# Forms of the first pair of batches: made at their first product instead of inside the attention, with a new instruction order

## The chip, the cores and the metric

One core of a Trainium2 chip runs the whole kernel as one program. The metric is device time in microseconds (us): the median of three runs. The engines named below are TensorE (PE; its weight loads are listed apart as PEld), VectorE (DVE), ScalarE (ACT), GpSimd (POOL) and SyncE (SP), which issues all transfers between DRAM and on-chip memory.

## What is computed

Sigmoid attention over 8 batches of 12 heads (448 positions, 64 wide), then per batch a low-rank mixing over positions and a two-layer channel network:

```python
scores = scale * np.matmul(q, k.transpose(0, 1, 3, 2)) - np.log(S)
attn = 1.0 / (1.0 + np.exp(-scores));  x = attn @ v        # heads side by side: 448 x 768 per batch
h = x.T @ U @ V                                            # rank 32
u = x + h.T
out = u + np.maximum(u @ w_ch1, 0.0) @ w_ch2               # 768 -> 3072 -> 768
```

## The kernel before

**Two stages on one TensorE.** The attention is cut into 24 *duos* (two head pairs of one batch). A duo `d` has seven score steps (group `S{d}`, line 509), each of four f32 matmuls of 64 x 64 into two PSUM banks, which ScalarE turns into a sigmoid (line 513), and seven value steps (`V{d}`, line 522). VectorE copies the result to a tile of `u` (line 533) and reduces its maximum (line 414). After three duos a batch `b` is *mixed*: its scale is found (`scale_of`, a 128 x 128 spread over the partitions on TensorE at line 390, with four small VectorE steps behind it), `u` is split into two f16 parts, transposed by a DMA (line 558), multiplied by U (seven matmuls, line 566; groups `M{b}0`, `M{b}1`) and by V (three matmuls, line 575; `N{b}0`, `N{b}1`), and VectorE adds that to `u`. Batches 0 and 1 stay on chip (`uu`); the others lie in `wt` until they are *parked* in DRAM.

**The channel network** multiplies two batches as a pair. The 2 x 2 block products are done with seven products instead of eight, so that both the weights and the inputs are needed in seven *forms* (sums and differences of blocks), each as a high and a low f16 part. One product is nine matmuls of 128 x 128 by 448 columns (line 749). An `in_quad` (group `X`) is the seven products of one unit of the first layer, with 16 VectorE steps on 128 x 448 behind them; an `out_quad` (`Y`) those of the second layer. There are 672 products. The pairs run in the order `SEGMENTS`: pair 0 with weight blocks 0 and 1, pair 1 with all four, pair 0 again with blocks 2 and 3, then pairs 2 and 3.

**Weight forms** are made once by `decode` (24 of them, groups `D{i}{n}`): integer words are loaded into `raw`, unpacked by ScalarE (line 607) and four VectorE steps (`tw<-raw`), scaled by a spread on TensorE (`ssw`, line 390), summed on GpSimd (line 623), split (ACT line 640, DVE `wt<-tw`), and stored to DRAM (`forms`). A product's weights come back from there into `wt` (1344 KB a load).

**Input forms** of a pair come from `u_form`: per chunk `c` of three, four GpSimd subtractions (line 684) give the differences 5, 6, 7 and 4, and each of the seven forms takes one ScalarE step (high part, line 680) and one VectorE step (low part, line 376, named `s_u__155` for pair 0). For pair 0 `first_forms` does this inside the attention, as soon as batches 0 and 1 are mixed, in seven form places and three temporary ones, and writes all 21 forms to DRAM (`ufar`). `forms_again` reads the 21 back at the end of the attention for the first segment, and once more for the third.

**Order.** Every step is recorded with a cost, what it reads and writes, and a wanted position; the dictionary `SHIFT` moves the position of each group. `Plan.order()` then makes one fixed list out of these, so each engine has its instructions in a set order and waits in it. Places for tiles are handed out in the same pass.

## Time and profile before

| | |
|---|---|
| median of 3 runs | 1491.05 us (1490.25 to 1492.3) |
| the profiled execution | 1495.41 us, of which its span is 1493.6 us |
| TensorE busy | 1461.9 us (98%) |
| VectorE busy | 1114.0 us (75%) |
| ScalarE busy | 646.9 us (43%) |
| GpSimd busy | 171.4 us (11%) |
| DRAM read / written | 234.09 MB / 59.87 MB |

The profile is of one execution. Busy time of TensorE is from the start of a matmul to its modelled end, and matmuls overlap; so the pace is read from the distance between starts. "Idle before" is the time in which an engine did nothing, put down to what ended it.

### The profile page before, as it was taken

The numbers are of one execution on the slowest core, as the hardware profiler recorded it, in microseconds if no ns is written. First come the engines' busy times: TensorE is split into PE (matmuls) and PEld (weight loads), VectorE is DVE, ScalarE is ACT, GpSimd is POOL, SyncE is SP. The second block draws the span as 40 slices with busy tenths as digits, with TensorE's granted clock in tenths as the row PEclk, the third lists the DMA queues.
The fourth block names the chain that finished last, engine by engine and source line by source line (L and its number), as shares of the span: only waits on it lengthen the run. The fifth ranks groups of instructions, "written<-read, shape, count | busy, mean of one in ns | idle before, by whom it ended". The sixth has DMA issues, their size and how long they took to land.

```text
span 1493.6 us, 22682 instructions
## 1 busy us (share of the span) xinstructions
PE 1461.9 (98%) x8934; PEld 718.1 (48%) x8934; DVE 1114.0 (75%) x1886; ACT 646.9 (43%) x925; POOL 171.4 (11%) x169
## 2 busy tenths in 40 slices
PE   8999999998999899999999999999999999999999
PEld 3333433344555455555555555555555555555554
DVE  3878898879999999996657668766565698666635
ACT  6988787755455455542204322431132335132200
POOL 1214122111214212210000021000000210000000
PEclk9999999999999999999999999999999999999999
DMA  8998999999769769744395367324333564233331
GB/s 278 258 279 284 266 315 284 295 277 311 255 225 357 271 219 307 251 159 149 117 338 192 111 228 253 129 72 147 134 112 111 210 234 143 80 111 132 110 129 74
DMA packets 207819, 306.46 MB, mean 205 GB/s; under 512 B 53344, under 2 KB 190688, under 8 KB 200032
## 3 DMA queue, kind: packets, MB, share of 16 engines
q1 hardware_dynamic: 207712, 305.01, 62.1%
q8 instruction: 70, 1.15, 0.3%
q14 instruction: 37, 0.30, 0.1%
HBM read 234.09 MB, written 59.87 MB: 197 GB/s over the span
## 4 chain that ended last, share of the span: by engine, by line
PE 85%; DVE 7%; DMA 4%; SPq 1%; ACT 1%; issue 1%; POOL 0%; DVEq 0%; ACTq 0%; POOLq 0%
PE banks L749 74%; PE banks L509 5%; PE banks L522 4%; DVE sp L376 2%; DMA sp<-q_in 2%; SPq L346 1%; DVE wt L376 1%; DMA raw<-w_in 1%; DVE tw L376 1%; DMA sp<-sp 1%; PE banks L566 0%; DMA parked<-wt 0%; ACT wt L640 0%; DVE uu L376 0%; DMA ufar<-sp 0%
## 5 line engine op out<-in xcount | busy, mean ns | idle before, releaser
L749 PE MATMUL banks<-sp,wt 128*128 128x448 f16 x5634 | 1092.6, 353 | 2.8 <-DVE sp L376 1.9
L749 PEld LDWEIGHTS <-wt 128*128 128x128 f16 x6048 | 592.4, 98 | 556.8 <-issue 8.3
L376 DVE SCALAR_TENSOR_TENSOR sp<-banks,fg,sp 128x448 f32<-128x448 f32 x206 | 138.7, 679 | 57.9 <-PE banks L749 55.8
L513 ACT ACTIVATE sp<-banks,bias_s 128x896 f32<-128x896 f32 x168 | 161.4, 1003 | 34.1 <-PE banks L509 33.8
L509 PE MATMUL banks<-sp 64*64 64x448 f32 x1344 | 159.7, 564 | 12.0 <-DMA sp<-q_in 7.5
L772 ACT ACTIVATE sp<-sp 128x448 f16<-128x448 f32 (+1 forms) x126 | 72.1, 574 | 220.3 <-DVE sp L376 217.7
L522 PE MATMUL banks<-sp 64*64 64x448 f32 x1344 | 149.1, 541 | 0.6 <-DVE wt L376 0.4
L623 POOL TENSOR_TENSOR tw<-tw 128x384 f32<-128x384 f32 x96 | 96.7, 1028 | 405.6 <-DVE tw L376 355.2
L376 DVE SCALAR_TENSOR_TENSOR sp<-sp 128x448 f32<-128x448 f32 (+1 forms) x191 | 118.2, 631 | 27.3 <-ACT sp L772 26.6
L786 ACT CAST sp<-sp 128x448 f16<-128x448 f32 x163 | 89.4, 564 | 87.4 <-DVE sp L376 56.4
L376 DVE SCALAR_TENSOR_TENSOR tw<-raw,tw 128x768 int32<-128x768 int32 x96 | 90.7, 954 | 10.7 <-ACT tw L607 9.5
L787 DVE TENSOR_TENSOR sp<-sp 128x448 f16<-128x448 f32 x163 | 96.0, 621 | 2.7 <-ACT sp L786 1.6
L509 PEld LDWEIGHTS banks<-sp 64*64 64x64 f32 x1344 | 52.9, 137 | 87.1 <-issue 47.2
L522 PEld LDWEIGHTS banks<-sp 64*64 64x64 f32 x1344 | 54.8, 134 | 67.4 <-issue 58.6
L791 ACT ACTIVATE sp<-banks,fg 128x448 f32<-128x448 f32 x42 | 26.4, 629 | 117.2 <-PE banks L749 117.0
L376 DVE SCALAR_TENSOR_TENSOR uu<-banks,kg__203,uu 128x448 f32<-128x448 f32 x60 | 40.5, 681 | 42.3 <-PE banks L749 41.9
L376 DVE SCALAR_TENSOR_TENSOR uu<-banks,kg__202,uu 128x448 f32<-128x448 f32 x60 | 40.5, 680 | 31.9 <-PE banks L749 31.0
L684 POOL TENSOR_TENSOR sp<-sp 128x448 f32<-128x448 f32 x23 | 28.7, 1266 | 289.3 <-DMA sp<-parked 288.6
L749 PE MATMUL banks<-tw,wt 128*128 128x448 f16 x252 | 60.7, 352 | 0.0
L772 ACT ACTIVATE sp<-banks,fg 128x448 f32<-128x448 f32 (+1 forms) x85 | 49.5, 627 | 24.7 <-PE banks L749 24.7
L607 ACT ACTIVATE tw<-raw,minus 128x768 f32<-128x768 uint16 x48 | 47.7, 1008 | 23.4 <-DVE wt L376 12.4
L376 DVE SCALAR_TENSOR_TENSOR uu<-banks,kg__201,uu 128x448 f32<-128x448 f32 x60 | 40.2, 679 | 21.4 <-PE banks L749 20.9
(272 smaller groups left out, 997.9 us busy)
## 6 DMA issues: line engine op xcount, KB each, us to landing
wt<-forms SPq DMA_DIRECT2D x96, 1344.0 KB, 6.5
forms<-wt SPq DMA_DIRECT2D x24, 1344.0 KB, 8.9
raw<-w_in SPq DMA_DIRECT2D x24, 768.0 KB, 6.8
raw<-w_in SPq DMA_DIRECT2D x48, 384.0 KB, 6.1
uu<-parked SPq DMA_DIRECT2D x48, 224.0 KB, 5.0
y_out<-uu SPq DMA_DIRECT2D x48, 224.0 KB, 2.5
sp<-k_in SPq DMA_DIRECT2D x47, 224.0 KB, 4.7
sp<-q_in SPq DMA_DIRECT2D x47, 224.0 KB, 4.8
```

Of the source, the lines that this page charges most:

```text
L376: nc.vector.scalar_tensor_tensor(out=out, in0=in0, scalar=s, in1=in1, op0=op0, op1=op1)
L509: nc.tensor.matmul(sc.x[rows_of(m), h, :S], t.x[r, 1, lo : lo + D], t.x[r, 0], start=True, stop=True)
L513: act(1.04, lambda c=c, sc=sc: nc.scalar.activation(a[c].x, sc.x[:, :, :S], AF.Sigmoid, bias=bias_s, scale=1.0 / math.sqrt(D)), [sc, "bias ...
L522: nc.tensor.matmul(av[m].x[rows_of(h), :S], vv.x[rows_of(m), m ^ x ^ 1, j, rows_of(h)], a[c].x[rows_of(m), h], start=c == 0, stop=c == 6, ...
L607: act(0.99, lambda out_=out_, low=low: nc.scalar.activation(out_(), low(), AF.Identity, bias=minus2, scale=-0.936 * 2.0 ** -35), kw + ["mi ...
L623: pool(1.08, lambda: nc.gpsimd.tensor_tensor(out=t.x[:, o], in0=t.x[:, x], in1=t.x[:, y], op=op_), kx, ko, pos + 2)
L684: pool(1.24, lambda: nc.gpsimd.tensor_tensor(out=o.x, in0=p_.x, in1=q_.x, op=ALU.subtract), [p_, q_], [o], pos)
L749: nc.tensor.matmul(bank.x[:, :S], wt[1](k, n, x), both(f)[:, y], start=start and k == i == 0, stop=k == 2 and i == 2, skip_group_check=True)
L772: act(0.57, lambda: nc.scalar.activation(o(), x(), AF.Relu, scale=sc), kx + [kf], ko, pos)
L786: act(0.57, lambda: nc.scalar.copy(both(f)[:, 0], x.x), [x], [(f, 0)], pos)
L787: dve2(0.63, lambda: nc.vector.tensor_tensor(out=both(f)[:, 1], in0=x.x, in1=both(f)[:, 0], op=ALU.subtract), [x, (f, 0)], [(f, 1)], pos)
L791: act(0.57, lambda: nc.scalar.activation(t.x, a.x[:, :S], AF.Copy, scale=s), [a, kf], [t], e)
```

## The change

The code of `u_form` is split into `u_form` (one form of one chunk) and `u_sub` (one subtraction). `first_forms` is no longer called after the second mixing. It is called where the first segment's products are laid out: the 12 subtractions are recorded there as early groups `Q5x`, `Q6x`, `Q7x`, `Q4x`, whose results are held in ten temporary places (`TEMP`, which were three, beside seven `FS`, now gone); the 21 forms (groups `T01`, `T06`, ...) are made after the tenth score step from the end, straight into places of the products; and the 21 writes to `ufar` (groups `Z`) follow. `forms_again` is left for the third segment alone. Further: where the early weight loads may go and what they wait for (`factors`), the places of `u` of batches 2 to 7, several costs that the planner uses, and all numbers of `SHIFT`.

```diff
-    mixing=-74.7, mixings=-110.3, W0s=-104.3, L0s=-107, W1s=-104.2, S0=-258.6, V0=13.4, L1s=-6.8, W2s=-45.5, S1=-204.3, V1=7.2, L2s=3, W3s=7.6,
+    mixing=-130.5, mixings=-34.9, W0s=-49.9, L0s=-49.1, W1s=-47.6, S0=-185.5, V0=-21.4, L1s=-14.3, W2s=-43.9, S1=-161.5, V1=259.7, L2s=-27.3,
...
-    TEMP = [at_("sp", (56 + i) * S, S) for i in range(3)]
-    FS = [at_("sp", (59 + i) * S, S) for i in range(7)]
+    TEMP = [at_("sp", (56 + i) * S, S) for i in range(10)]
...
-        u32s[b] = [plan.tile(f"u{b}{c}", [UU[b * NP + c]]) if b < 2 else plan.tile("u2", U2) for c in range(NP)]
+        u32s[b] = [plan.tile(f"u{b}{c}", [UU[b * NP + c]]) if b < 2 else plan.tile("u2", U2[b % 2 * NP : b % 2 * NP + NP], False) for c in range(NP)]
...
+    def u_form(fs, n, c, src, su, pos, after=()):
+        f = fs[n, c] = spot("uf")
+        act(0.66, lambda: nc.scalar.activation(both(f)[:, 0], src.x, AF.Copy, scale=su.x), [src, su], [(f, 0)], pos, after)
+        dve2(0.68, lambda: rest(both(f)[:, 1], src.x, su.x, both(f)[:, 0]), [src, su, (f, 0)], [(f, 1)], pos)
...
-    def first_forms(su, pos):
-        for c in range(3):
-            plan.group = f"T0{c}"
-            x = {(r, n): u32s[n][c + 3 * r] for r in range(2) for n in range(2)}
-            fs = {}
-            u_form(fs, c, x, su, pos + 4 * c, FS, TEMP)
-            for n in range(1, 8):
+    def first_forms(su, early, pos, after):
+        fs, t = {}, {}
+        x = {(c, r, n): u32s[n][c + 3 * r] for c in range(3) for r in range(2) for n in range(2)}
+        for i, n in enumerate((5, 6, 7, 4)):
+            for c in range(3):
+                plan.group = f"Q{n}{c}"
+                o = t[n, c] = plan.tile("ut0", TEMP)
...
+        for i, n in enumerate((1, 6, 7, 5, 2, 4, 3)):
+            plan.group = f"T0{n}"
+            for c in range(3):
+                src = {1: x[c, 0, 0], 2: x[c, 1, 0], 3: x[c, 1, 1]}.get(n) or t[n, c]
+                u_form(fs, n, c, src, su, pos + 2 * i, after)
+        for n in (1, 6, 7, 5, 2, 4, 3):
+            plan.group = f"Z{n}"
+            for c in range(3):
                 f = fs[n, c]
-                load(lambda n=n, c=c: ufar[:, n - 1, c], lambda f=f: f.x, P * S * 4, [(f, 0), (f, 1)], [("ufar", n, c)], pos + 4 * c + 1.0)
+                load(lambda n=n, c=c: ufar[:, n - 1, c], lambda f=f: f.x, P * S * 4, [(f, 0), (f, 1)], [("ufar", n, c)], pos + 60.0)
+        return fs
...
-    def factors(i, n, e, pos, after):
-        wt = plan.tile("wt", near[0], False)
+    def factors(i, n, e, pos):
+        wt = plan.tile("wt", near[0] if len(begun) > 7 else WT[1:3] if begun else WT[1:2], False)
+        after = begun[-21:-20] or (valued[-1:] if len(begun) > 7 else valued[-3:-2] if begun else scored[-WTS : len(scored) - WTS + 1])
...
-            first_forms(su, at + 7.0)
...
+        elif opening:
+            fs = first_forms(su, at - 150.0, at - LEAD, scored[-AGAIN : len(scored) - AGAIN + 1])
```

What it moves, at three places. VectorE in the middle of the attention, before the change (`s_u__155` marks a form's low part, `wt<-banks` the copy of a value step's result, `mx` its maximum):

```order
L376 SCALAR_TENSOR_TENSOR sp<-uu,s_u__155,sp 128x448
L376 SCALAR_TENSOR_TENSOR sp<-sp,s_u__155 128x448
L376 SCALAR_TENSOR_TENSOR sp<-uu,s_u__155,sp 128x448
L414 TENSOR_REDUCE mx__159<-wt 128x1
L376 SCALAR_TENSOR_TENSOR sp<-uu,s_u__155,sp 128x448
L376 SCALAR_TENSOR_TENSOR sp<-sp,s_u__155 128x448 x2
L533 COPY wt<-banks 128x448
```

VectorE at the end of the attention, after the change (`kap` marks the addition of a mixing, `s_x` a mixing's split, `32x384` the step between U and V of a mixing):

```order
L533 COPY wt<-banks 128x448
L376 SCALAR_TENSOR_TENSOR sp<-wt,s_x__136,sp 128x448
L376 SCALAR_TENSOR_TENSOR sp<-uu,s_u__155,sp 128x448 x6
L376 SCALAR_TENSOR_TENSOR sp<-sp,s_u__155 128x448 x2
L414 TENSOR_REDUCE mx__187<-wt 128x1
L533 COPY wt<-banks 128x448
L414 TENSOR_REDUCE mx__187<-wt 128x1
L376 SCALAR_TENSOR_TENSOR wt<-banks,kap__141,wt 128x448
L414 TENSOR_REDUCE mx__173<-wt 128x1
L376 SCALAR_TENSOR_TENSOR sp<-sp,s_u__155 128x448
L376 SCALAR_TENSOR_TENSOR sp<-uu,s_u__155,sp 128x448 x3
L376 SCALAR_TENSOR_TENSOR sp<-sp,s_u__155 128x448 x9
```

The 21 low parts, which stood among the copies of batches 2 and 3, now stand in two blocks among those of the last duos. ScalarE has them likewise: 18 in a row behind the sigmoid of the 158th score step, then three more.

TensorE at the end of the attention, before the change (`wt` products, `ssw` a decode's spread, `mm_x__128` the spread of the last batch's mixing):

```order
L749 MATMUL banks<-sp,wt 128x448
L522 MATMUL banks<-sp 64x448 x20
L390 MATMUL banks<-ident,ssw__117 128x128
L390 MATMUL banks<-ident,mm_x__128 128x128
L749 LDWEIGHTS wt
```

TensorE at the same place after the change:

```order
L762 MATMUL banks<-sp,wt 128x448
L390 MATMUL banks<-ident,ssw__117 128x128
L522 MATMUL banks<-sp 64x448 x8
L509 MATMUL banks<-sp 64x448 x8
L522 MATMUL banks<-sp 64x448 x20
L762 LDWEIGHTS wt
```

The two spreads directly behind the last value steps are gone from there: the decode's stands before the last nine attention steps, the last batch's behind eleven more products. In all TensorE changes between 64-row and 128-row matmuls 93 times after the change and 109 times before it.

SyncE at the end of the attention, before the change:

```order
L346 DMA sp<-ufar 128x448 x7
L558 DMA_TRANSPOSE sp<-sp 128x21x128 x2
L346 DMA sp<-ufar 128x448 x14
L346 DMA raw<-w1_in 128x3x128 x4
L346 DMA parked6<-wt 128x448 x6
```

and after it:

```order
L558 DMA_TRANSPOSE sp<-sp 128x21x128
L346 DMA ufar<-sp 128x448 x8
L346 DMA parked5<-wt 128x448
L346 DMA ufar<-sp 128x448 x12
L558 DMA_TRANSPOSE sp<-sp 128x21x128
L346 DMA ufar<-sp 128x448
```

At this place 21 reads of `ufar` have become 21 writes; the 21 writes of the middle of the attention are gone.

## Rows read from the trace of the kernel before

**Rows 1.** The page: busy time of each engine over the span.

```profile
PE 1461.9 (98%) x8934; PEld 718.1 (48%) x8934; DVE 1114.0 (75%) x1886; ACT 646.9 (43%) x925; POOL 171.4 (11%) x169
```

**Rows 2.** Busy time by stretch: from:to, length, engines, granted clock, DMA.

```profile
0.00:110.00 110.00, 101.39 (x951) 40.34 (x955) 73.42 (x136) 85.64 (x95) 20.50 (x29) 1.00 0.95 273
110.00:180.00 70.00, 65.66 (x597) 26.94 (x593) 59.61 (x108) 59.12 (x77) 23.07 (x20) 0.95 0.91 285
180.00:290.00 110.00, 106.78 (x1004) 42.43 (x1000) 94.08 (x167) 90.68 (x102) 23.12 (x24) 1.00 1.02 282
290.00:350.00 60.00, 52.43 (x389) 20.59 (x388) 49.68 (x101) 33.77 (x44) 12.23 (x12) 0.91 0.96 328
350.00:480.00 130.00, 129.48 (x689) 67.36 (x688) 124.78 (x206) 65.79 (x95) 25.63 (x24) 1.00 0.82 267
480.00:530.00 50.00, 46.22 (x243) 23.62 (x242) 45.88 (x79) 27.10 (x40) 13.87 (x13) 1.00 0.79 289
530.00:1493.00 963.00, 959.93 (x5078) 496.79 (x5075) 666.55 (x1094) 284.81 (x476) 53.04 (x48) 1.00 0.47 163
```

**Rows 3.** TensorE's timeline where pair 0's forms are made: start, length, idle before.

```profile
168.77 0.32 PE L390 MATMUL banks<-ident,mm_x__127 128*128 128x128 f32 x1 [0.90 <-DVE wt L376]
170.68 4.83 PE L509 MATMUL banks<-sp 64*64 64x448 f32 x24 [1.59 <-DMA sp<-q_in]
...
176.30 1.73 PE L509 MATMUL banks<-sp 64*64 64x448 f32 x16
177.80 0.97 PE L522 MATMUL banks<-sp 64*64 64x448 f32 x8
```

**Rows 4.** Forms, subtractions and sigmoids between 110 and 165 us: busy, mean ns.

```profile
L376 DVE SCALAR_TENSOR_TENSOR sp<-sp,s_u__155 128x448 f16<-128x448 f32 x12 | 8.7, 747 | 0.0
L376 DVE SCALAR_TENSOR_TENSOR sp<-uu,s_u__155,sp 128x448 f16<-128x448 f32 x9 | 8.2, 907 | 0.0
...
L684 POOL TENSOR_TENSOR sp<-uu 128x448 f32<-128x448 f32 x6 | 8.3, 1376 | 18.7 <-DVE uu L376 14.9 <-DVE sp L376 3.6
...
L513 ACT ACTIVATE sp<-banks,bias_s 128x896 f32<-128x896 f32 x30 | 29.1, 1002 | 3.7 <-PE banks L509 3.6
L680 ACT ACTIVATE sp<-sp,s_u__155 128x448 f16<-128x448 f32 x12 | 7.7, 661 | 0.1
L680 ACT ACTIVATE sp<-uu,s_u__155 128x448 f16<-128x448 f32 x9 | 5.9, 662 | 1.0 <-DVE s_u__155 L397 1.0
```

**Rows 5.** The same VectorE step for pair 2, beside no subtractions (880 to 925 us).

```profile
L376 DVE SCALAR_TENSOR_TENSOR sp<-sp,s_u__183 128x448 f16<-128x448 f32 x13 | 8.2, 679 | 0.0
```

**Rows 6.** TensorE's timeline: the waits at the end of the attention.

```profile
294.40 0.98 PE L509 MATMUL banks<-sp 64*64 64x448 f32 x8 [2.05 <-ACT sp L513]
...
342.31 0.32 PE L390 MATMUL banks<-ident,ssw__117 128*128 128x128 f32 x1 [2.72 <-ACT tw L615]
345.03 0.48 PE L390 MATMUL banks<-ident,mm_x__128 128*128 128x128 f32 x1 [2.40 <-DVE mm_x__128 L419]
```

**Rows 7.** VectorE between 290 and 350 us, by kind of step.

```profile
L376 DVE SCALAR_TENSOR_TENSOR sp<-wt,s_x__136,sp 128x448 f16<-128x448 f32 x6 | 5.0, 840 | 0.0
L533 DVE COPY wt<-banks 128x448 f32<-128x448 f32 x8 | 4.9, 615 | 2.1 <-PE banks L522 2.1
L376 DVE SCALAR_TENSOR_TENSOR wt<-banks,kap__139,wt 128x448 f32<-128x448 f32 x6 | 4.1, 677 | 0.9 <-PE banks L575 0.9
L414 DVE TENSOR_REDUCE mx__187<-wt 128x1 f32<-128x448 f32 x6 | 3.7, 614 | 0.1
L376 DVE SCALAR_TENSOR_TENSOR wt<-tw,s_w__125,wt 128x1152 f16<-128x1152 f32 (+1 forms) x2 | 3.2, 1608 | 0.0
```

**Rows 8.** TensorE's timeline around a spread and a mixing.

```profile
94.20 0.32 PE L390 MATMUL banks<-ident,mm_x__128 128*128 128x128 f32 x1 [0.33 <-DVE mm_x__128 L419]
...
108.51 0.66 PE L566 MATMUL banks<-sp,ua 128*128 128x384 f16 x3
```

**Rows 9.** The page: DMA issues, size, median us from issue to landing.

```profile
wt<-forms SPq DMA_DIRECT2D x96, 1344.0 KB, 6.5
```

More of the change, by code (lines that the diff above doesn't have):

```diff
@@ L360, in dve2, with act @@
         op("DVE", max(0.06, cost - 0.08), fn, reads, writes, pos, land=0.12, port=True)
-    def act(cost, fn, reads, writes, pos):
-        op("ACT", max(0.06, cost - 0.1), fn, reads, writes, pos, land=0.14)
+    def act(cost, fn, reads, writes, pos, after=()):
+        op("ACT", max(0.06, cost - 0.1), fn, reads, writes, pos, land=0.14, after=after)
     def pool(cost, fn, reads, writes, pos, after=()):
@@ L511, in duo @@
                 kq = ([qa] if 0 in hs else []) + (list(qb) if 1 in hs else [])
-                scored.append(pe(0.757, score, [(t, i) for t in kq for i in range(2)], [sc, (a[c], "place")], pos, modes=(64, 64)))
-            act(1.04, lambda c=c, sc=sc: nc.scalar.activation(a[c].x, sc.x[:, :, :S], AF.Sigmoid, bias=bias_s, scale=1.0 / math.sqrt(D)), [sc, "bias"], [a[c]], pos)
+                scored.append(pe(0.752, score, [(t, i) for t in kq for i in range(2)], [sc, (a[c], "place")], pos, modes=(64, 64)))
+            act(0.99, lambda c=c, sc=sc: nc.scalar.activation(a[c].x, sc.x[:, :, :S], AF.Sigmoid, bias=bias_s, scale=1.0 / math.sqrt(D)), [sc, "bias"], [a[c]], pos)
         plan.group = f"V{d}"
@@ L527, in duo @@
             late = at + VALUES + V_STEP * c
-            x = pe(0.757, lambda c=c: values(c), [a[c]] + [(vv, x) for x in range(3)] + (av if c else []), av, late, modes=(64, 64), after=prev)
+            x = pe(0.752, lambda c=c: values(c), [a[c]] + [(vv, x) for x in range(3)] + (av if c else []), av, late, modes=(64, 64), after=prev)
         valued.append(x)
@@ L566, in mixed @@
                     nc.tensor.matmul(tp.x[:, :384], m.rearrange("p a b -> p (a b)"), x[:, j], start=j == 0, stop=j == 6)
-            pe(1.2, mixed, [(xt, i) for i in range(3)] + ["ux"] + KUA, [tp], pos + 2.0)
+            pe(1.14, mixed, [(xt, i) for i in range(3)] + ["ux"] + KUA, [tp], pos + 2.0)
             act(0.5, lambda tp=tp, tt=tt: nc.scalar.activation(tt.x, tp.x[:, :384], AF.Copy, scale=DOWN), [tp], [tt], pos + 2.0)
@@ L707, in u_forms @@
                 x[r, n] = t
-            u_form(fs, c, x, su, at, None, None)
-        return fs
-    def first_forms(su, pos):
-        for c in range(3):
-            plan.group = f"T0{c}"
-            x = {(r, n): u32s[n][c + 3 * r] for r in range(2) for n in range(2)}
-            fs = {}
-            u_form(fs, c, x, su, pos + 4 * c, FS, TEMP)
-            for n in range(1, 8):
+            t1, t2, t3, t4 = (spot("ut") for _ in range(4))
+            u_sub(t1, x[0, 1], x[0, 0], at)
+            u_form(fs, 1, c, x[0, 0], su, at)
@@ new lines, in u_forms @@
+            u_form(fs, 5, c, t1, su, at)
+            u_sub(t2, x[1, 1], t1, at)
+            u_form(fs, 6, c, t2, su, at)
+            u_sub(t3, x[1, 1], x[0, 1], at)
+            u_form(fs, 7, c, t3, su, at)
+            u_form(fs, 2, c, x[1, 0], su, at)
+            u_sub(t4, x[1, 0], t2, at)
+            u_form(fs, 4, c, t4, su, at)
+            u_form(fs, 3, c, x[1, 1], su, at)
+        return fs
+    def first_forms(su, early, pos, after):
[5 more added lines that the diff above has]
+                o = t[n, c] = plan.tile("ut0", TEMP)
+                if n == 5:
+                    u_sub(o, x[c, 0, 1], x[c, 0, 0], early + 9 * i + 3 * c)
+                elif n == 6:
+                    u_sub(o, x[c, 1, 1], t[5, c], early + 9 * i + 3 * c)
+                elif n == 7:
+                    u_sub(o, x[c, 1, 1], x[c, 0, 1], early + 9 * i + 3 * c)
+                else:
+                    u_sub(o, x[c, 1, 0], t[6, c], pos + 10)
+        for i, n in enumerate((1, 6, 7, 5, 2, 4, 3)):
[6 more added lines that the diff above has]
+            for c in range(3):
```

125 lines of the change are left out of this document (54 added, 71 removed).

## Prediction

> **What bounds the kernel now.** I read the page first, for the busy shares. TensorE is busy 98% of the span [rows 1], so the kernel is a list of matmuls, and only what keeps them apart can be won. The same 672 products, 24 duos and 16 half mixings run after the change; nothing of this work is removed.
>
> Next, the busy time by stretch, to see where the other 2% lies [rows 2]. From 530 us on TensorE is idle for 963.00 - 959.93 = 3.1 us, and that is the end of the program. There 5078 matmuls take 959.93 us, 0.189 us each and 1.70 us for a product of nine: a floor. All that can be won lies before 530 us: idle 8.6 us up to 110 (part of it ahead of the first matmul), 4.3 between 110 and 180, 3.2 up to 290, 7.6 between 290 and 350, 0.5 up to 480, 3.8 up to 530. Two stretches also show less than the full granted clock. 0.95 over 70 us means (1 - 0.95) x 2 x 70 = 7 us at the lower level, 1.2 GHz, which cost half of that, 3.5 us, if TensorE had work throughout; 0.91 over 60 us means some 10.8 us at 1.2 GHz, at most 5.4 us. In both, TensorE had waited just before [rows 3, 6].
>
> Last, TensorE's timeline and the other engines in those stretches, for who was waited for. Between 110 and 180 us VectorE is busy 59.6 us of 70 and ScalarE 59.1 [rows 2]. TensorE waits there for VectorE steps, 0.90 us, and for a late q, 1.59 us [rows 3]. In this stretch stand the 21 forms: on VectorE 8.7 + 8.2 = 16.9 us, on ScalarE 7.7 + 5.9 = 13.6 us, and GpSimd's subtractions [rows 4]. At the end of the attention TensorE waits 2.05 us for a sigmoid, and 2.72 and 2.40 us at two spreads whose inputs ScalarE and VectorE had not finished [rows 6]. From 350 to 480 us VectorE is busy 124.8 of 130 us, 96% [rows 2]: there it is nearly a second bound.
>
> **The change part by part.** Signs are for the time: minus is a gain.
>
> *The forms leave the middle of the attention.* 16.9 us of VectorE and 13.6 us of ScalarE go from a stretch where both are 85% busy, and 21 writes of 0.23 MB with them. That stretch loses 4.3 us idle and 3.5 us to the clock, 7.8 us in all [rows 2]. The 1.59 us for q [rows 3] may stay. The twelve subtractions stay in the attention. I take -6; bounds -7.8 and 0 (another late step in the same place).
>
> *They come back at the end of the attention.* I count the new order of VectorE from the spread of batch 6's mixing to the first addition behind a product, with these rows' prices: 21 forms at 8.2/13 = 0.63 us, 13.2 [rows 5]; 4 copies and 8 reductions at 0.61, 7.4; 4 additions of mixings at 0.68, 2.7; 6 splits at 0.83, 5.0; a decode's two splits, 3.2 [rows 7]; small steps, about 2. Together 33 us. TensorE's part between the same two marks is 24 attention steps at 0.75 us (two of them start 1.50 us apart [rows 3]), 18.0 us, one product, 1.7 us, and the matmuls of a mixing and eight changes of shape, some 3: 23 us. So TensorE has to wait up to 10 us here. It needs not all of VectorE's list: the first thing that it cannot do without is the step between the two parts of batch 6's mixing, which stands behind the last form, 26 us down the list and 19 us down TensorE's: a wait of 7. ScalarE says the same: 18 forms in a row at 13.6/21 = 0.65 us are 11.7 us in which no sigmoid (29.1/30 = 0.97 us [rows 4]) is made, and the value steps of the last but one duo wait for two of these. A wait of 7 us and a stretch at 1.2 GHz behind it like those in the profile, worth 1.7 to 3.4 us, make 9.5 us. What goes from the same place: 7.6 us idle [rows 2] and about 4 for the clock (part of its 5.4 fell in idle time), since the two spreads that were waited for for 2.72 and 2.40 us [rows 6] now have nine attention steps or eleven products ahead of them. Net -2; bounds -8 (VectorE gets ahead, no wait) and +2 (the full 10 us).
>
> *What VectorE owes afterwards.* In the new order five more decodes are done by the 69th product, where there were three. By VectorE's list up to the 69th product, priced like this, it has some 17 us more to do than TensorE from batch 6's spread on, and before the change some 6; the wait at the end of the attention pays 7 to 10 of the 17, and what is left may lie beside products that need none of it. Against this, the waits between 480 and 530 us, 3.8 us [rows 2], stood where decodes were late, and with earlier decodes they have no cause. I take 0; bounds -4 and +7.
>
> *Fewer changes of shape.* 93 for 109. The row of a single spread lasts 0.32 us [rows 6], and of a spread with its way there and back some 0.3 to 0.4 is lost; half of that for each of 16 is 2.4 to 3.2 less the spreads themselves, which remain. I take -1.5; bounds 0 and -3.
>
> *Mixings sit closer.* From a mixing's spread to its first matmul the shortest case in the trace took 14.3 us, with no wait at its end [rows 8]. In the new order four of eight mixings have only about 12 us of TensorE's work between these two. Scales, splits and the transposing DMA must fit in there; if 14.3 us is what they need, each costs 2.3. I take +2; bounds 0 and +9. Behind these matmuls attention steps of the same list wait.
>
> *Transfers.* SyncE's queue loses 21 writes in the attention and has 21 writes instead of 21 reads at its end: 4.8 MB less of some 80 so far, 17 us of transfer at 285 GB/s [rows 2]. What stands behind the writes in the queue is the load of the second unit's weights, which can be issued only when the first unit's seventh product has freed the place. It lands after 6.5 us [rows 9]; nine attention steps, 6.8 us, cover it. If that cover were gone it would cost its 6.5 us. I take 0.
>
> Sum: -6 - 2 + 0 - 1.5 + 2 + 0 = -7.5 us. It is made against the profiled execution (1495.41 us, span 1493.6), which took 4.4 us more than the median; the terms are differences, so I take them from the median: 1491.05 - 7.5 = **1483.5 us**.
>
> **A rule weighed.** The low parts that are made beside GpSimd's subtractions take longer: 0.907 and 0.747 us there [rows 4] against 0.679 for the same step where no subtraction runs [rows 5]. The Trainium skill's page "SBUF — State Buffer", section "Who interferes with whom", says that VectorE instructions with two inputs on chip and GpSimd instructions that read on-chip memory exclude each other for a whole instruction. The traces agree: 21 x 0.679 = 14.3 against 16.9 us, so that 2.6 us of waiting sit in 21 steps. By that page the moved forms become cheaper, as ten of the twelve subtractions stay behind, and these would then hold up decodes and mixings instead; with the skill's rule the burst above is 13 us, with the dearer row, 0.907, it would be 19, and the wait at the end of the attention 12 instead of 7.
>
> **The rivals.** *The burst and the debt decide (slower).* The 21 forms fall where VectorE is next to full. Price: all of the 10 us wait and 3.4 for the clock at the end, the 7 of the 17 us owed by the 69th product that this wait does not pay, the closer mixings at +6: -6 + 2 + 7 - 1.5 + 6 = +7.5, and so 1498.5 us. It decides as soon as VectorE's list is more than about 8 us longer than TensorE's there. For it: 96% from 350 us on [rows 2]. Against: TensorE waited in the same place before [rows 6], and those waits go. *The waits only change places (same).* The order is new everywhere; the stretch of the forms is relieved, but other late q's and closer mixings take its 6 us: 1491 us. For it: TensorE's waits outside that stretch, 8.6 us up to 110 and 3.2 up to 290 [rows 2], are not due to forms. *Nearly all waits go (much faster).* Relieved by 17 us, VectorE is ahead when the burst comes: -7.8 - 6 - 1.5 = -15, so 1476 us. Against it: the count of the burst. That the change does not do what it says can be left out: the order shows the forms moved.
>
> **How the numbers follow.** Forecast 0.50, slower rival 0.19, same 0.16, much faster 0.15. The likeliest is 1483.5 us. Its own bounds, one wide term at a time, are 1477 to 1490. The range reaches toward the rivals until 0.1 is left out on either side: 1474 to 1497. A measurement of this kernel can tell 0.2%, 3 us, from no change: faster means below 1488. Nearly all of the forecast and all of the much faster case lie there, 0.64; within 3 us, 0.17; slower, 0.19.
>
> **What would show it.** Right: between 110 and 180 us VectorE well below 59 us busy, no lower clock there, waits below 2 us; at the end of the attention one wait of 5 to 8 us for VectorE or ScalarE with forms in front of it; no wait at the two spreads; about 31 us of TensorE's idle time down to 24. Wrong: a TensorE wait above 10 us at the forms, further waits in the first 70 products, waits at the first matmul of the mixings, or any wait beyond 530 us, where there is none now.

## The result and the profile after

The changed kernel is slower by 1%: 1506.93 us (median of 6, 1503.4 to 1513.34) against 1491.67 us for the kernel before in the same runs, a ratio of 1.0104, 95% interval [1.0081, 1.0127]. The forecast was 1483.5 us, range 1474 to 1497. The profiled execution of after took 1513.34 us (span 1511.6), the longest of its six; that of before 1495.41 (span 1493.6). A run of almost the same order, further down (r0), left a profile of 1508.19 us; where the two differ much, both are given.

Busy time of after by stretch, columns as in [rows 2], whose first six stretches are the same:

```profile
0.00:110.00 110.00, 99.56 (x928) 39.39 (x929) 71.73 (x135) 82.80 (x92) 22.40 (x29) 0.98 0.92 260
110.00:180.00 70.00, 68.12 (x647) 27.75 (x649) 60.48 (x108) 58.37 (x66) 24.05 (x22) 1.00 0.94 285
180.00:290.00 110.00, 101.01 (x924) 41.02 (x920) 82.26 (x146) 81.60 (x92) 19.37 (x20) 0.97 1.02 273
290.00:350.00 60.00, 53.26 (x426) 22.45 (x419) 55.66 (x100) 47.00 (x66) 13.02 (x12) 0.94 0.87 277
350.00:480.00 130.00, 118.07 (x597) 59.25 (x596) 118.53 (x214) 59.44 (x86) 23.36 (x23) 0.96 0.77 241
480.00:530.00 50.00, 49.75 (x265) 25.69 (x263) 43.92 (x72) 25.11 (x39) 21.37 (x16) 1.00 0.88 319
```

Set TensorE's idle time (length minus busy) beside [rows 2]: -2.5 us between 110 and 180, where the forms were made; +1.8 up to 110, +5.8 between 180 and 290, -0.8 up to 350, +11.4 between 350 and 480, -3.5 up to 530. That is +12.2 us. From 530 us on it is +1.6, nearly all of it one wait for VectorE that before did not have; apart from that both run at the floor there:

```profile
937.32 7.54 PE L762 MATMUL banks<-sp,wt 128*128 128x448 f16 x39 [1.47 <-DVE uu L376]
```

The rest of the 18.0 us between the two spans, 4.2 us, is the clock: TensorE is busy 1466.1 us instead of 1461.9 with the same matmuls. The trace shows 27.3 us at 1.2 GHz after the start of the program, in five stretches that each follow waits, where before had 17.1 in three; TensorE had work in 22.2 and 13.6 of them.

TensorE's waits in after (line, what it waited for: total us, times, longest); before had 7.5 us on the first line, 1.9 on the second (line 566, a transpose), none on the third and the fifth, 0.9 on the fourth, and 27.8 us in all where after has 41:

```profile
PE banks L509 <- DMA sp<-q_in: 10.2, 5, 4.4
PE banks L566 <- DMA sp<-sp: 9.4, 6, 4.2
PE banks L762 <- DMA wt<-forms: 5.4, 5, 1.4
PE banks L575 <- DVE sp L376: 4.4, 1, 4.4
PE banks L575 <- DVE wt L533: 3.0, 2, 2.8
```

Five places are behind most of this. First, a mixing that waits for its transpose, on TensorE's timeline (start, length, idle before it). The stretch at 1.2 GHz is the 6.8 us from 271.4 on; the 16 score matmuls that it ends in take 2.17 us instead of 1.68:

```profile
273.34 1.14 PE L566 MATMUL banks<-sp,ua 128*128 128x384 f16 x3 [4.24 <-DMA sp<-sp]
...
277.25 2.17 PE L509 MATMUL banks<-sp 64*64 64x448 f32 x16
...
286.73 1.68 PE L509 MATMUL banks<-sp 64*64 64x448 f32 x16
```

Second, SyncE's queue. At the same place two transposes hold it for 10.77 us (first row), and k and q for a later duo are issued only behind them; nobody waited for these. At 80 us TensorE did wait, for a q that was issued behind two transposes (SyncE's queue, then TensorE):

```profile
262.84 10.77 SPq L558 DMA_TRANSPOSE sp<-sp  x2
...
53.09 6.17 SPq L558 DMA_TRANSPOSE sp<-sp  x1
62.08 5.57 SPq L558 DMA_TRANSPOSE sp<-sp  x1
73.35 0.46 SPq L346 DMA_DIRECT2D sp<-q_in  x1
80.09 1.82 PE L509 MATMUL banks<-sp 64*64 64x448 f32 x8 [2.41 <-DMA sp<-q_in]
```

Third, the forms at the end of the attention: the copy out of a bank (line 533, at 311.23) stands on VectorE behind eight forms (`s_u__155`), and TensorE waits for it:

```profile
308.72 0.36 PE L575 MATMUL banks<-vst,sp 128*128 128x448 f16 x1
311.90 0.35 PE L575 MATMUL banks<-vst,sp 128*128 128x448 f16 x1 [2.82 <-DVE wt L533]
313.15 1.12 PE L566 MATMUL banks<-sp,ua 128*128 128x384 f16 x3 [0.90 <-DVE wt L376]
...
316.30 1.77 PE L509 MATMUL banks<-sp 64*64 64x448 f32 x8 [0.76 <-ACT sp L513]
```

```profile
305.94 3.66 DVE L376 SCALAR_TENSOR_TENSOR sp<-uu,s_u__155,sp 128x448 f16<-128x448 f32 x6
309.51 1.28 DVE L376 SCALAR_TENSOR_TENSOR sp<-sp,s_u__155 128x448 f16<-128x448 f32 x2
310.70 0.61 DVE L414 TENSOR_REDUCE mx__187<-wt 128x1 f32<-128x448 f32 x1
311.23 0.62 DVE L533 COPY wt<-banks 128x448 f32<-128x448 f32 x1
```

Fourth, the products around the 30th. TensorE waits for their VectorE and ScalarE steps, then for weights, and 6.8 us at 1.2 GHz begin at 394.3:

```profile
391.33 0.54 PE L762 MATMUL banks<-sp,wt 128*128 128x448 f16 x2 [0.50 <-DVE sp L800]
392.47 0.35 PE L762 MATMUL banks<-sp,wt 128*128 128x448 f16 x1 [0.59 <-ACT sp L799]
393.48 0.54 PE L762 MATMUL banks<-sp,wt 128*128 128x448 f16 x2 [0.66 <-DVE sp L800]
395.30 11.53 PE L762 MATMUL banks<-sp,wt 128*128 128x448 f16 x45 [1.28 <-DMA wt<-forms]
```

Fifth, the mixing of the last batch, which now stands at products 48 to 53 instead of 16 to 24. Its second step waits 4.38 us for the mixing's middle, which ScalarE copies only at 436.64, when a product's VectorE step has left the place (second fence), and which VectorE then finishes at 437.17. The product behind it waits for its weights:

```profile
431.52 1.87 PE L762 MATMUL banks<-sp,wt 128*128 128x448 f16 x9
437.77 0.74 PE L575 MATMUL banks<-vst,sp 128*128 128x448 f16 x3 [4.38 <-DVE sp L376]
439.29 4.93 PE L762 MATMUL banks<-sp,wt 128*128 128x448 f16 x18 [0.77 <-DMA wt<-forms]
```

```profile
436.64 0.49 ACT L569 ACTIVATE sp<-banks 128x384 f16<-128x384 f32 x1 [0.88 <-DVE sp L791]
```

To compare runs at the same point of the work and not of the clock, take from the start of a matmul what all matmuls before it need unhindered (0.094, 0.115, 0.163 or 0.189 us by kind). What is left is the time lost so far, in us, in each profiled execution:

| TensorE's work done, us | before | after | r0 | what lies before it |
|---|---|---|---|---|
| 150 | 29.7 | 27.1 | 26.8 | the stretch that made the forms |
| 260 | 45.5 | 46.7 | 43.8 | attention up to the forms' new place |
| 330 | 56.7 | 61.4 | 58.5 | end of the attention, products up to the 30th (before: the 28th, with the last mixing) |
| 400 | 56.6 | 76.7 | 73.5 | products up to the 69th (after, r0: with the last mixing) |
| 600 | 61.0 | 77.2 | 73.4 | products up to the 186th |

So up to the 30th product r0 is 1.8 us behind before, and after 4.7. Then 15 us are lost up to the 69th product, in the fourth and fifth place, where before loses nothing. Behind that before loses 4.4 us and the new order next to nothing.

### The profile page after: what moved, and what is told of

Its sections match the earlier page's. It is cut to its first block, busy times and chain, and to the rows that moved or that the text cites. A ratio compares the mean times of both kernels' runs of the same rounds, so it can differ in the third digit from the quotient of the medians.

```text
span 1511.6 us, 22651 instructions
## 1 busy us (share of the span) xinstructions
PE 1466.1 (97%) x8934; PEld 720.5 (48%) x8934; DVE 1114.9 (74%) x1886; ACT 648.0 (43%) x925; POOL 178.6 (12%) x169
## 4 chain that ended last, share of the span: by engine, by line
PE 78%; DMA 9%; DVE 8%; ACT 3%; issue 1%; SPq 1%; POOL 0%; DVEq 0%; ACTq 0%; POOLq 0%
PE banks L762 67%; PE banks L509 5%; PE banks L522 4%; DMA sp<-sp 3%; DMA wt<-forms 3%; DVE sp L376 2%; DMA sp<-q_in 1%; DVE wt L376 1%; DVE tw L376 1%; SPq L346 1%; DVE uu L376 1%; PE banks L566 1%; ACT sp L676 1%; DMA sp<-parked 1%; DMA parked<-wt 1%
## 5 line engine op out<-in xcount | busy, mean ns | idle before, releaser
L376 DVE SCALAR_TENSOR_TENSOR sp<-banks,fg,sp 128x448 f32<-128x448 f32 x200 | 135.0, 679 | 64.7 <-PE banks L762 62.8
L785 ACT ACTIVATE sp<-sp 128x448 f16<-128x448 f32 (+1 forms) x119 | 68.2, 575 | 253.8 <-DVE sp L376 225.7
L509 PE MATMUL banks<-sp 64*64 64x448 f32 x1344 | 163.0, 557 | 11.0 <-DMA sp<-q_in 10.2
L522 PE MATMUL banks<-sp 64*64 64x448 f32 x1344 | 152.5, 543 | 2.2 <-DMA sp<-v_in 1.2
L376 DVE SCALAR_TENSOR_TENSOR tw<-raw,tw 128x768 int32<-128x768 int32 (+1 forms) x97 | 93.2, 969 | 8.6 <-ACT tw L607 5.2
L509 PEld LDWEIGHTS banks<-sp 64*64 64x64 f32 x1344 | 55.1, 136 | 83.9 <-issue 50.4
L522 PEld LDWEIGHTS banks<-sp 64*64 64x64 f32 x1344 | 57.2, 134 | 72.8 <-issue 60.7
L785 ACT ACTIVATE sp<-banks,fg 128x448 f32<-128x448 f32 (+1 forms) x91 | 53.4, 628 | 36.2 <-PE banks L762 36.2
L762 PE MATMUL banks<-tw,wt 128*128 128x448 f16 x234 | 56.7, 352 | 0.0
```

Of the source, the lines that this page charges most:

```text
L376: nc.vector.scalar_tensor_tensor(out=out, in0=in0, scalar=s, in1=in1, op0=op0, op1=op1)
L509: nc.tensor.matmul(sc.x[rows_of(m), h, :S], t.x[r, 1, lo : lo + D], t.x[r, 0], start=True, stop=True)
L522: nc.tensor.matmul(av[m].x[rows_of(h), :S], vv.x[rows_of(m), m ^ x ^ 1, j, rows_of(h)], a[c].x[rows_of(m), h], start=c == 0, stop=c == 6, ...
L762: nc.tensor.matmul(bank.x[:, :S], wt[1](k, n, x), both(f)[:, y], start=start and k == i == 0, stop=k == 2 and i == 2, skip_group_check=True)
L785: act(0.57, lambda: nc.scalar.activation(o(), x(), AF.Relu, scale=sc), kx + [kf], ko, pos)
```

## The experiments

All edits are to the changed kernel with its order kept, unless said; y3, y4 and z2 are made on the order of r0. Diff lines without code in them are in words. Ratios are to the kernel before in the same runs (1492.19 to 1494.06 us).

**Three suspects, each cut.** e1: the forms (VectorE's part a constant); e2: the transposes; e3: the weights; e4: all three.

```diff
-dve2(0.68, lambda: rest(both(f)[:, 1], src.x, su.x, both(f)[:, 0]), ...)
+dve2(0.68, lambda: nc.vector.memset(both(f), 0.5), ...)                       # e1, and 16 columns on ScalarE
-dma_start_transpose(out=xt.x, in_=xs.x...)
+dma_start_transpose(out=xt.x[:, :7], in_=xs.x...[:, :2 * S])                  # e2, batches 0 to 5
-load(lambda: wt.x, lambda: forms[0][n], ...)
+load(lambda: wt.x[:, :2 * FORMW // 7], lambda: forms[0][n][:, :2 * FORMW // 7], ...)   # e3
```

> The changed kernel in its own order, with the 21 forms of pair 0 cut down where they are made: ScalarE copies 16 columns instead of 448, VectorE fills the form with a constant. (The output is not the reference's; all transfers stay.) Theory T (transfers land later than the order supposes, at mixings and at weights): only the wait that stood behind the forms goes, 2.82 + 0.90 + 0.76 us and half of a 6.83 us stretch at 1.2 GHz, about 7.5 us of some 1507: 1499. Theory B (the forms at the end of the attention cost all of it): the whole difference to the kernel before goes, 1491 or less, and the waits between 330 and 450 us go too.

> The changed kernel in its own order, with the transposes of batches 0 to 5 cut to one of three chunks (the rest of the mixing's input is zero or old data, so the output is not the reference's). Theory T: of the 9.4 us for which TensorE waits for transposes, 8.6 fall on these batches and go, with about 5 us for the stretches at 1.2 GHz at 80 and 271 us: 1507 falls by 9 to 13, to 1494 to 1498. Theory B: these waits are covered by others that follow, 1504 or more.

> The changed kernel in its own order, with the first weight loads of the products cut to a seventh of their bytes wherever the place already holds weights (stale weights are used, so the output is not the reference's). Theory T: the 5.4 us of waits for weights between 349 and 440 us go, with up to 3.4 us for the stretch at 1.2 GHz at 394 us: 1507 falls by 5 to 9, to 1498 to 1502. Theory B: weights are late only because VectorE is: the wait moves to VectorE, 1505 or more.

> All three cuts at once. If the three causes add up: 7.5 + 11 + 7 = 25 us, so 1482, below the kernel before (1491). If they only take turns (each wait hidden behind the next), 1491 to 1497.

Measured: e1 1511.91 us, 1.0132 [1.0108, 1.0156]; e2 1491.6, 0.9989 [0.9977, 1.0001]; e3 1508.03, 1.0100 [1.0075, 1.0124]; e4 1497.02, 1.0026 [1.0012, 1.0041]. Cutting the transposes gains as much as the change had lost, cutting the weights nothing. That the loss lies in the transposes does not follow: the kernel before gains from the same cut (b1, below). e1 did not test what it should: the constant takes VectorE longer than the step that it replaced. VectorE's timeline of e1 at the forms; eight take 7.39 us, 0.92 each, where six of after's took 3.66, 0.61 each (above):

```profile
303.45 7.39 DVE L684 MEMSET sp<- 128x896 f16 x8
310.76 0.56 DVE L414 TENSOR_REDUCE mx__187<-wt 128x1 f32<-128x448 f32 x1
311.24 0.61 DVE L533 COPY wt<-banks 128x448 f32<-128x448 f32 x1
```

(The Trainium skill's page "VectorE: DVE Perf Modes", section "Zero memsets can be issued as uint32 (trn2)", says that a memset takes one cycle per element whatever the type. The trace has 896 elements in 0.92 us, 1.03 ns each, in one type alone; that the type makes no difference no run here shows.) So e1 made the row of forms longer, and TensorE's longest wait for line 533 grew from 2.8 to 5.5 us, its waits for it in all from 3.0 to 10.3. That fits e1 and e4, which came out 4 to 6 us above after and e2.

**Is it the order or the transfers?** b1 is e2's cut in the kernel *before*. r0, r1 and r3 leave nothing out: with all tiles in their places, the list is played once more, each engine taking the ready instruction that came first in the old order. In r0 the costs are the planner's (it moves one transpose), in r1 each transpose lands 1.5 us later, in r3 also VectorE takes the copies of the last three duos first.

```diff
-        for i in self.order():
+        for i in self.settle(self.order()):
...
+                told = pipe + o[6] + (later if o[9][1] else 0.0)
```

> The kernel BEFORE, its order unchanged, with the transposing transfers of batches 0 to 5 cut to one of their three chunks (so two thirds of what the mixings of those batches read is wrong data). The same cut in the changed kernel took 15 us away. Theory T (order): the cut is worth much only where the order puts the mixing's matmuls close behind the transfer, 12 to 15 us of TensorE work in the changed kernel and 15 to 25 us here; so the kernel before gains 0 to 4 us, 1488 to 1493 us, and its waits for a transpose (1.9 us in all) and its half-clock stretches at 169, 295 and 343 us stay. Theory L (load): the transfers cost every order alike, by the time they hold the issuing queue and the memory; then it gains as much as the changed kernel did, 10 to 15 us, 1478 to 1483 us.

> The changed kernel with its orders and the places of all its tiles kept, but for one transposing transfer (of a batch in the middle of the attention) that is issued two loads earlier, and one decode step on ScalarE that changes places with a copy beside it; it is the base for the next two, which are made in the same way. All theories: the changed kernel's time within 4 us, 1503 to 1510 us; a gain of more than that would say that the one transfer was the worst of them.

> The changed kernel, nothing left out and every tile in the same place, its instructions put in order once more with the same priorities but with each transposing transfer supposed to land 1.5 us later. TensorE's work between the spread of a batch and its first mixing matmul becomes 12.7, 15.0, 13.2, 13.5, 15.3, 15.0, 12.0 and 51.5 us instead of 12.0, 13.5, 11.7, 11.7, 14.5, 15.0, 12.0 and 51.5. Theory T (order): the waits of the mixings for the transposes (9.4 us in the changed kernel) and the half-clock stretches behind them (80 and 271 us) go for the most part, 7 to 13 us: 1494 to 1500 us. Theory L (load): the transfers are the same, so no gain, 1503 to 1510 us.

> As the run with the mixings later, with one more change: around 305 us, on VectorE, the copies of the last three attention steps out of the banks stand ahead of the 21 forms of the first pair instead of between and behind them (they were 8 us behind their products at worst). Nothing is left out. Theory B (burst): the wait of TensorE at 309 to 316 us (4.5 us) and the half-rate stretch behind it (3.4 us) go: 4 to 8 us below the run with the mixings later, 1487 to 1494 us. Rival: the products of the first pair then wait for the forms that were put back, and nothing is gained: within 2 us of the run with the mixings later. If theory B holds, the earlier cut of the forms didn't gain because the memset that took the place of a form's low part took 0.92 us instead of 0.60, so that the burst was 6 us longer, not shorter: its loss of 4 us was the price of that.

Measured: b1 1485.49 us, 0.9956 [0.9942, 0.9969]; r0 1506.18, 1.0092 [1.0076, 1.0107]; r1 1505.11, 1.0083 [1.0070, 1.0097]; r3 1506.93, 1.0089 [1.0074, 1.0103]. The kernel before gains 6.7 us from the cut, the changed one 15 to 17 (from r0's 1.0092 or after's 1.0104 to 0.9989): the transposes cost some 10 us more in the new order. With the cut in both, e2 is still 0.33% or 5 us slower than b1. But r1 speaks against it being only the distance to the mixing. Its waits for transposes are 1.8 us instead of 9.4, and up to 260 us of work it has lost 35.8 us instead of r0's 43.8 (second table below); from there to 600 it loses 33.4 where r0 loses 29.6, and the medians differ by 1 us. In r3 the wait at the forms moved on, from the copies to the corrections of batch 5, which stood behind the same eight forms:

```profile
307.24 1.12 PE L566 MATMUL banks<-sp,ua 128*128 128x384 f16 x3 [4.11 <-DVE wt L376]
```

**Further cuts, further orders.** y1: VectorE's part of the forms an f16 copy (0.28 us). x1: r1's order with the steps of mixings and copies first from batch 5 on, on VectorE and ScalarE, nothing left out; x2 and x4: x1 with e3's and e2's cut.

```diff
-dve2(0.68, lambda: rest(both(f)[:, 1], ...), ...)
+dve2(0.68, lambda: nc.vector.tensor_copy(both(f)[:, 1], both(f)[:, 0]), ...)   # y1
+first[i] -= 8.0 for VectorE's and ScalarE's ops of V21-V23, M5-M7, N5-N7       # x1, x2, x4
```

> The changed kernel, orders kept, with the low part of the first pair's 21 forms made by a plain f16 copy of the high part (so those forms are wrong), which should take VectorE 0.2 to 0.4 us each instead of 0.60: the burst at 306 to 321 us is really shorter this time, by 4 to 8 us, where the first cut had made it 6 us longer. Theory B (burst): the wait of TensorE at 309 to 316 us (4.5 us) and its half-rate stretch (3.4 us) go or shrink to a third: 4 to 8 us less than the changed kernel, 1499 to 1503 us. Rival: the wait is passed on to the next transfer or copy, the time stays at 1505 to 1508 us.

> As the run with the mixings later (1505 us), and from batch 5 on VectorE and ScalarE take the steps of a mixing, its corrections and the copies of the last three attention steps ahead of the 21 forms and of the products' steps as soon as they can be done. Nothing is left out. In the run with only the copies first the wait had moved on to the corrections of batch 5 (4.1 us behind 8 forms, 4.9 us of work); here 4 forms stand ahead of them, 2.4 us. Theory B: of the 34 us that TensorE loses after the 260th us of its work (15 in the kernel before) the burst's 8 and the last mixing's 8 shrink by half or more: 1490 to 1500 us. Rival (the sum is fixed): VectorE and ScalarE are the bound there, whatever comes first, and another wait takes the place: 1502 to 1507 us.

> As the run with the chain first, and the first 18 loads of the products' weights cut to a seventh where the place already held weights (the products are wrong). The cut alone had gained nothing. Theory: the waits change places as long as the others stand, so with the others shortened the cut now gains its 4 to 5 us of waits for weights (at 340 to 440 us): 4 to 6 us below the run with the chain first. Rival: the weights never set the time, within 2 us of it.

> As the run with the chain first, and the transposing transfers of batches 0 to 5 cut to one of three chunks (the mixings read wrong data). In the changed kernel the cut gained 15 us, 16 of it before the 260th us of TensorE's work; the mixings put later took 8 to 11 us of these away. If the two cure the same waits, the cut gains only 4 to 7 us more here (as it gained 6.7 in the kernel before): 1484 to 1495 us. If the transfers cost by themselves, it gains 10 to 15 us again: 1476 to 1488 us.

Measured: y1 1507.51 us, 1.0078 [1.0057, 1.0098]; x1 1503.84, 1.0058 [1.0043, 1.0072]; x2 1502.01, 1.0046 [1.0031, 1.0061]; x4 1491.95, 0.9984 [0.9973, 0.9995]. y1 is inconclusive: VectorE's short copies now waited, one by one, for ScalarE's high parts, so that TensorE waited 2.68 us for the copy out of the bank instead of 2.82 (VectorE's timeline of y1):

```profile
306.88 0.28 DVE L677 COPY sp<-sp 128x448 f16<-128x448 f16 x1 [0.28 <-ACT sp L676]
...
310.41 0.61 DVE L533 COPY wt<-banks 128x448 f32<-128x448 f32 x1
```

x1 gains 0.25% on r1, less than expected: another wait, 3.8 us for the middle of the mixing behind fifteen forms on ScalarE, took the place of the old ones. x2 gains 2 us on x1, too little to tell. x4 gains 11 us on x1: with the mixings later, the cut of the transposes still gains two thirds of what it did.

**The last two places by themselves, and all together.** y2: the forms are constants, high part by GpSimd, low part a VectorE copy. z1: GpSimd writes both. y3: the middle of the last mixing in a place that is free earlier, its steps first, nothing left out. y4: y2, y3 and e2's cut. z2: z1, y3, e2's and e3's cut. y5: x1 with y3's place.

```diff
-act(0.66, lambda: nc.scalar.activation(both(f)[:, 0], src.x, AF.Copy, scale=su.x), ...)
+act(0.66, lambda: nc.gpsimd.memset(both(f), 0.5), ...)            # z1; y2: [:, 0] alone
-dve2(0.68, lambda: rest(both(f)[:, 1], ...), ...)
+dve2(0.68, lambda: None, ...)                                      # z1; y2: tensor_copy(both(f)[:, 1], vst)
+t.got = the slot of `sp` that had been out of use longest                    # y3, for `tt` of batch 7
```

> The changed kernel, orders kept, but the first pair's 21 forms are not made: the high part is a constant written by GpSimd, the low part an f16 copy of a constant on VectorE (0.28 us instead of 0.60); ScalarE has nothing to do for them (21 times 0.56 us before). Theory B2 (the burst is on ScalarE and VectorE together, in order, and the copies, corrections and sigmoids of the last steps stand behind it): TensorE's stop at 309 to 316 us (4.5 us) and the half-rate stretch behind it (3.4 us) go: 5 to 8 us less, 1498 to 1502 us. Rival: the stop is set by something else (a place, a transfer), 1504 to 1508 us.

> The changed kernel with the middle of the last batch's two mixings in a place that nothing used shortly before, and with the steps of this mixing taken first on ScalarE and VectorE, as soon as they can be done; all else as it was (but for the one transfer of the base run, 1506 us). Nothing is left out. The copy of the mixing's middle moves ahead of one form on ScalarE and its low part ahead of five steps on VectorE (3.4 us). Theory: the wait at 437.8 us (4.4 us) falls to some 1.4 us and half of the half-rate stretch behind it goes: 3 to 6 us less, 1500 to 1503.5 us. Rival: the weights that arrive at 439.3 us are late next, and it gains at most 1.5 us.

> The two cuts of the forms' making and of the last mixing as in the two runs before, and the transposing transfers of batches 0 to 5 cut to a third. If these three are the loss and add up: 15 + 6 + 4 us less than the changed kernel, 1478 to 1486 us. If they only change places with other waits (weights, loads of q): above 1488 us.

> The run with the chain first (1504 us), the last mixing's middle in its own place as well; nothing is left out. Theory: 2 to 5 us less than that run, 1499 to 1502 us, still above the kernel before by 0.3 to 0.6%. Rival: as that run, 1503 to 1505 us.

> The changed kernel, orders kept; the first pair's 21 forms are constants that GpSimd alone writes, VectorE and ScalarE do nothing for them (12.8 and 11.8 us less work between 304 and 322 us). Theory B2: the copy out of the bank follows its product at once, the stop at 309 to 316 us (4.5 us) and the half-rate stretch behind it (3.4 us) go: 5 to 8 us less than the changed kernel (1506.5 us), 1498 to 1502 us. Rival: the stop stays or another takes its place, 1504 to 1508 us; then the burst is not what the loss is made of.

> As the run before, with the last mixing's middle in its own place and its steps first, the transposing transfers of batches 0 to 5 cut to a third, and the first 18 loads of weights cut to a seventh. If these four are the loss: 15 + 7 + 4 + 4 us less than the changed kernel, 1474 to 1482 us, below what the kernel before takes with its transposes cut (1485.5 us). If something else in the new order costs time, it stays above 1485 us.

Measured: y2 1506.5 us, 1.0084 [1.0069, 1.0099]; y3 1507.82, 1.0097 [1.0080, 1.0115]; y4 1493.05, 0.9998 [0.9987, 1.0010]; y5 1502.97, 1.0063 [1.0049, 1.0077]; z1 1501.31, 1.0054 [1.0036, 1.0073]; z2 1483.74, 0.9935 [0.9919, 0.9950].

y2 did not shorten the row either, for another reason: the second of VectorE's copies lasted 4.49 us, until GpSimd had ended a subtraction and eight constants in a row, at 310.09. The six behind it took 0.26 us each, 0.19 from start to start. TensorE's wait for line 533 grew to 4.86 us. VectorE, then GpSimd, in y2:

```profile
305.74 4.49 DVE L677 COPY sp<-vst 128x448 f16<-128x448 f16 x1
310.14 1.19 DVE L677 COPY sp<-vst 128x448 f16<-128x448 f16 x6
```

```profile
305.64 1.15 POOL L682 TENSOR_TENSOR sp<-uu,sp 128x448 f32<-128x448 f32 x1
306.71 3.38 POOL L676 MEMSET sp<- 128x448 f16 x8
```

(The Trainium skill's page "SBUF — State Buffer", section "SBUF: two separate sides", calls the port pair that VectorE's fast copies share with GpSimd an exclusive lock, held for a whole instruction. The trace agrees that one waits for the other, and the wait was longer here: one copy of 0.26 us waited for nine GpSimd instructions, 4.49 us. The prediction weighed this for the subtractions only.)

z1 is the clean cut. The waits for line 533 are gone (0.2 us left), and the time falls by 0.5% (5 to 7 us). What was late next is a transpose again:

```profile
307.69 0.66 PE L566 MATMUL banks<-sp,ua 128*128 128x384 f16 x3 [2.58 <-DMA sp<-sp]
```

y3 shortened the wait it aimed at (4.38 to 1.27 us) and gained nothing, since the weights were late next (timeline of y3):

```profile
425.42 0.74 PE L576 MATMUL banks<-vst,sp 128*128 128x448 f16 x3 [1.27 <-DVE sp L376]
430.13 4.98 PE L763 MATMUL banks<-sp,wt 128*128 128x448 f16 x18 [3.97 <-DMA wt<-forms]
```

z2, with all four cut, is 25 us below after (1.0104 to 0.9935), 2 us above what was expected, and 3 us below b1, the old order with the transposes cut alone. The 25 us are about the sum of the single cuts (by their ratios e2 17, z1 7.5, y3 and e3 1 each or less): the four do not hide one another's cost. It has one stretch at 1.2 GHz, 3.4 us, where after had five. Its stretches, as above:

```profile
290.00:350.00 60.00, 58.12 (x373) 28.62 (x374) 51.60 (x98) 33.58 (x45) 20.57 (x21) 1.00 0.74 247
350.00:480.00 130.00, 119.29 (x615) 60.17 (x613) 117.83 (x206) 60.66 (x90) 30.87 (x29) 0.99 0.58 174
```

Up to 350 us hardly anything is lost. Between 350 and 480, 10.7 us of idle time stay, with the transposes, weights and forms all out of the way; there VectorE and ScalarE are waited for in small pieces (0.4 to 2.0 us) at products and at the last mixing. The time lost at the same points of the work, in us:

| TensorE's work done, us | b1 | e2 | r1 | z1 | z2 |
|---|---|---|---|---|---|
| 150 | 22.9 | 20.6 | 22.8 | 24.1 | 19.9 |
| 260 | 34.1 | 30.6 | 35.8 | 42.5 | 27.1 |
| 330 | 46.0 | 43.6 | 51.1 | 51.9 | 33.8 |
| 400 | 46.0 | 57.0 | 66.7 | 65.6 | 46.5 |
| 600 | 50.4 | 58.5 | 69.2 | 65.7 | 48.9 |

Between 330 and 400 every run of the new order in the two tables loses 12.7 to 15.6 us, and neither of the old order any; the least was x2's 9.3. No run cured that part, so it belongs to the new order itself, where the last mixing stands among the products and VectorE's steps around it; that these two are the whole cause is argued, not shown. Which step of the order would have to move is open. Not tested either is the move of the forms by itself: the change also moves all of `SHIFT`, the places of weights and of `u`, and no run has the forms moved in the old order.

## Why the prediction was wrong, step by step

Against the terms of the sum stand what the stretches show: the change in idle time, and in half of the time at 1.2 GHz in which TensorE had work. The division is rough, since the new order also moves work between stretches; together the five make the 18 us between the spans.

| term | forecast, us | measured, us |
|---|---|---|
| the forms leave the attention (110 to 180) | -6 | -5.0 |
| they come back (290 to 350) | -2 | -2.4 |
| mixings sit closer (up to 110, 180 to 290) | +2 | +11.7 |
| what VectorE owes, transfers (350 to 530) | 0 | +12.2 |
| behind 530 | 0 | +1.6 |

**The forms leave the attention: -6. The size came out, one of its reasons did not.** Idle 1.9 instead of 4.3 us between 110 and 180, and full clock instead of 0.95. But VectorE was to be well below 59 us busy there, and it was busy for 60.5: decodes took the forms' place, ten unpacking steps (`tw<-raw`) where five had been. So the waits went without VectorE being relieved, and why is not shown.

**They come back: -2, bounds -8 and +2. Right within its bounds, in the main for the reasons given.** TensorE stopped for 2.82 + 0.90 + 0.76 = 4.5 us at the forms (7 was forecast) with a stretch at 1.2 GHz, and the two spreads of [rows 6] were not waited for any more. What it waited for first was a copy out of a bank behind eight forms; the middle of batch 6's mixing behind the last form, which I had named, was not waited for. z1 gives the row of forms its price: 5 to 7 us.

**Mixings sit closer: +2, bounds 0 and +9. The mechanism was right, the size wrong.** I took the 14.3 us of [rows 8] as what a mixing needs, which made 2.3 us for each of four, and put 2 us of these 9 into the sum. The transposes then made single waits of up to 4.24 us, 9.4 in all, and had two effects with no term in the sum: the queue that they hold (the 2.41 us for q at 80 us; of the waits for q, 10.2 us in after and 7.5 in before, e2's cut leaves 6.4) and the stretches at 1.2 GHz. Up to 290 us that is 7.6 us of idle time outside the forms' stretch, and 4.1 for the clock. It ate what the forms had set free. By the cuts the transposes cost 15 to 17 us in the new order, 6.7 in the old one; how much of it is the distance and how much the queue is not settled, since r1 removed most of the waits and x4 still gained 11.

**What VectorE owes: 0, bounds -4 and +7, and transfers: 0. Here the forecast failed.** The waits after 480 us went as I said (3.8 to 0.25), but between 350 and 480 the idle time rose by 11.4 us and the clock fell to 0.96. I counted VectorE's list up to the 69th product, as a whole, let TensorE's wait for the forms pay 7 to 10 of its 17 us, and let the rest lie beside products that need none of it. They needed it: around the 30th product, and at the last batch's mixing. I had seen that mixing move behind eleven more products, but not asked what it meets there, at products 48 to 53: a step that TensorE needs at once stands behind steps of the products. VectorE need not be full for that; it was busy 91% of this stretch, less than before (96%). And the load of the second unit's weights, which I had covered with nine attention steps by its usual 6.5 us, landed 10.3 us after its issue and was waited for all the same (1.43 us); later loads have no such cover, and the waits for weights came to 5.4 us in all. The two lines, of SyncE and TensorE:

```profile
339.52 0.32 SPq L346 DMA_DIRECT2D wt<-forms  x1
349.82 6.99 PE L762 MATMUL banks<-sp,wt 128*128 128x448 f16 x36 [1.43 <-DMA wt<-forms]
```

**Fewer changes of shape: -1.5.** Not told apart by any run.

**The rule weighed.** It came out: away from the subtractions each moved low part took 0.68 us, and three unpacking steps of decodes that now lie beside subtractions (from 129.65 us on) took 1.12, 1.89 and 1.78 us, the seven others in that stretch 0.95 or 0.96.

**The signs.** Of those that I had named for "wrong", three came: further waits in the first 70 products, waits at the first matmul of mixings, and the one beyond 530 us. TensorE's idle time went from 31 us to 45.5, not to 24.

**The rivals.** What came is nearest to "the burst and debt decide" (1498.5 us), and 8 us above it. Its parts were there, the wait at the forms at less than half its 10 us, the closer mixings and the clock dearer than its +6. Its chance, 0.19, was too low: three terms of mine had their upper bounds at +2, +9 and +7, and these are not independent. One late list makes all of them late, and the longer waits each brought a stretch at half the clock.

## What to carry to other kernels

An order that is packed closer moves waits as well as work: beside the stretch that is relieved, list every step whose distance to its producer shrank, and price each with the longest landing in the trace, the queue time behind it and the slower clock after the wait. A cut of one wait can show nothing because the next late thing takes over (r3, y3), so cut the suspects together as well, compare the result with the sum of the single cuts, and read the time lost at equal points of the work: here it showed a part of the loss that no suspect holds. Make the same cut in the kernel before, too: without b1 the transposes would have passed for the whole cause. See that a cut really shortens the step: three of the four cuts of the forms did not shorten their row.

## What was not expected of the hardware

A transpose holds SyncE's queue for most of the time until it lands, and shrinking it shortens the one far more than the other. Of the 16 transposes, issue takes 3.2 to 7.3 us in after (first row, ns: least, median, most). With twelve of them cut to a third the median falls from 4.54 to 1.27 us (second row, e2), but the median time from issue to landing only from 6.7 to 5.8 us:

```profile
L558 SPq DMA_TRANSPOSE sp<-sp x16: 3157/4538/7258, 53.1 to 433.1; - x16
```

```profile
L558 SPq DMA_TRANSPOSE sp<-sp x16: 1221/1270/7282, 53.0 to 412.6; - x16
```

A constant of 896 columns cost VectorE more than a two-input step on 448 (0.92 against 0.61 us). A single f16 copy, 0.26 us by its neighbours, was held for 4.49 us beside a row of GpSimd instructions.
